# Six runs of V-products for each group of heads become five, with one head scored alone before and after a run

## The chip, the cores and the metric

The kernel runs on one core of a Trainium2 chip. The metric is the device time of one execution in microseconds (us). The core's engines run at the same time and meet at semaphores: TensorE (PE, matmuls into the accumulation banks, eight of 128 x 512 float32), ScalarE (ACT), VectorE (DVE), GpSimd (POOL), and SyncE (SP), which issues DMA transfers.

## The reference: one transformer block, cut to what matters

```
h  = x + Attn(layernorm(x))          # 2048 tokens, D = 512, 32 query heads of 16
h2 = h + FFN(layernorm(h))           # F = 1792, gelu gate

Attn: q = x @ wq (32 heads), k = x @ wk, v = x @ wv (one k, v for all heads)
      p = softmax(q k^T / 4);  o = p @ v;  o @ wo
FFN:  (gelu(x @ w_gate) * (x @ w_up)) @ w_down
```

All arrays are float32. Every query attends to every key.

## The kernel before: what is tiled, staged and ordered

**Attention.** The queries are cut into 4 blocks of 512 tokens, the heads into 8 groups of four, the keys into 16 chunks of 128. For each block, group and chunk there are four scored heads. They are scored in pairs (`scores`, L363): two matmuls with 50 contraction rows each, one in rows 0 to 63 and one in rows 64 to 127 of the array, side by side, into a tile `s` of two banks. ScalarE turns the pair into exponentials with one instruction on 128 x 1024 elements (L374) and writes them into a buffer `p` of the chunk; there are five such buffers. When both pairs of a chunk are done, the V-products (`weigh`, L376) multiply the four heads by the chunk's V, 32 columns wide, side by side into one bank `acc` that collects the 16 chunks of a group. Each V-product is float32 and shows as two matmuls, so a chunk has eight.

A group of heads is thus 32 pairs and 16 chunks; the whole has 1024 pairs and 512 chunks. `n` counts pairs.

**Dense products.** The projection with wo (`pp`), gate and up (`pg`, `pu`) and down (`pd`) of a finished block run between the attention matmuls of the next block (`queue_products`, `rows`, L808). A weight or activation is split in a high and a low part, so a product has three matmuls for each piece of the contraction. The contraction of 128 rows is cut in two halves of 64: the first halves (`firsts`, rows 0 to 63) and the second halves (`seconds`, rows 64 to 127) are two lists of matmuls. One `step` (L837) issues the next of each, side by side, into two different banks; the seconds run `LAG` = 6 steps behind the firsts. A product of 12 or more steps ends with an addition or a copy on VectorE (`done`), which frees the bank, and then up to two further pieces of waiting VectorE work are issued (`side(2)`: the gelu gate, layer norm, transposes). There are three banks for the dense products: one with the firsts, one with the seconds, one being freed or free.

**The order.** TensorE, ScalarE and GpSimd execute in the order in which the program is written, and in the stage of this change VectorE and SyncE too. First comes a prologue with k, v and the first q, then a lead (pairs 0 to 278, loops at L1125 and L1127), in which attention runs beside the remaining q projection and the weights' splitting; there the score tiles have three buffers, later two. After pair 279 the table `CYCLES` sets the order: one entry is (how many chunks a run of V-products takes, the pattern of `s` for a pair and `d` for a step after that run, the pattern when there is no dense work). Three entries make 8 chunks, 16 pairs and 36 steps. Each cycle begins with `before` (tanh instructions, two pieces of side work, a transpose of a normed tile) and `finish(count)`, the run of V-products; then the pattern follows. When the dense list has fewer steps ready than the pattern wants (`idle`), what is ready is issued at once, `catch_up` lets the lone seconds run to their end if the next product is a `pg` or none is left, and the cycle goes on in the third pattern: runs of one chunk with two pairs between them. Such a cycle is called plain here, the other woven. A dense product that starts after a catch-up has its first six firsts alone.

Behind the last run of V-products comes a tail: the last block's projection and feed-forward layer.

## Time and profile before

| what | value |
|---|---|
| three runs | 1395.55, 1395.99 (median), 1398.74 us |
| the profiled execution | 1397.61 us, its span 1395.8 us |
| PE busy | 1379.5 us, 99% of the span |
| ACT busy | 1034.1 us, 74% |
| DVE busy | 651.0 us, 47% |
| granted TensorE clock | 1.000 |
| first dense matmul, last V-product's end | 313.5 us, 1253.6 us |

A timeline row gives the start in us from the span's start, the length in us, the engine, the line, the operation with output and inputs, and how many instructions were merged. Matmul ends are modelled, so the distance between two starts is the safer number. A "step" or a "pair" stands for two matmuls in the two halves of the array.

### The profile page before, as it was taken

The numbers are of one execution on the slowest core, as the hardware profiler recorded it, in microseconds if no ns is written. First come the engines' busy times: TensorE is split into PE (matmuls) and PEld (weight loads), VectorE is DVE, ScalarE is ACT, GpSimd is POOL, SyncE is SP. The second block draws the span as 40 slices with busy tenths as digits, with TensorE's granted clock in tenths as the row PEclk, the third lists the DMA queues.
The fourth block names the chain that finished last, engine by engine and source line by source line (L and its number), as shares of the span: only waits on it lengthen the run. The fifth ranks groups of instructions, "written<-read, shape, count | busy, mean of one in ns | idle before, by whom it ended". The sixth has DMA issues, their size and how long they took to land.

```text
span 1395.8 us, 25287 instructions
## 1 busy us (share of the span) xinstructions
PE 1379.5 (99%) x10406; PEld 753.3 (54%) x10406; DVE 651.0 (47%) x1097; ACT 1034.1 (74%) x1157; POOL 239.8 (17%) x346
## 2 busy tenths in 40 slices
PE   9999999999999999999999999999999999999998
PEld 7533333325555555545555555545555555558886
DVE  7413131314354444548364444448364453546665
ACT  8799999997787777877787777787778777772000
POOL 7576777621000000002000000001000000011000
PEclk9999999999999999999999999999999999999999
DMA  5565776753232333311522433321433333233552
GB/s 163 167 216 184 235 235 233 220 181 133 73 106 74 118 104 103 116 60 46 181 94 81 134 103 103 104 66 31 148 103 104 118 103 103 91 123 126 187 205 94
DMA packets 66783, 180.32 MB, mean 129 GB/s; under 512 B 9672, under 2 KB 9672, under 8 KB 66628
## 3 DMA queue, kind: packets, MB, share of 16 engines
q1 hardware_dynamic: 55324, 143.29, 31.0%
q0 software_dynamic: 10208, 35.26, 7.6%
q8 instruction: 84, 1.38, 0.4%
q14 instruction: 39, 0.32, 0.1%
q10 hardware_dynamic: 1128, 0.07, 0.1%
HBM read 130.87 MB, written 47.45 MB: 128 GB/s over the span
## 4 chain that ended last, share of the span: by engine, by line
PE 94%; ACT 2%; DMA 1%; DVE 1%; issue 1%; SPq 0%; POOL 0%; ACTq 0%; POOLq 0%
PE acc L378 33%; PE s L370 20%; PE pg L827 9%; PE pu L827 8%; PE pd L827 7%; PE pq L219 3%; PE pd L865 3%; PE pg L865 3%; PE pu L865 3%; PE pp L827 2%; ACT p L374 2%; PE pp L929 1%; PE pd_rest L877 1%; DMA x<-in_A_x_dram 1%; PE pk L1327 1%
## 5 line engine op out<-in xcount | busy, mean ns | idle before, releaser
L374 ACT ACTIVATE p<-s 128x1024 f32<-128x1024 f32 x1024 | 959.6, 1037 | 223.7 <-PE s L370 220.6
L378 PE MATMUL acc<-p,v_sb 128*32 128x512 f32 x4096 | 490.0, 598 | 0.0
L370 PE MATMUL s<-qg,kaug 50*128 50x512 f32 x1984 | 388.3, 426 | 4.2 <-ACT p L374 4.1
L370 PEld LDWEIGHTS s<-qg,kaug 50*128 50x128 f32 x1984 | 169.4, 184 | 281.7 <-ACT p L374 123.5
L378 PEld LDWEIGHTS acc<-p,v_sb 128*32 128x32 f32 x4096 | 108.7, 109 | 233.1 <-issue 218.7
L827 PE MATMUL pg<-x2h,w 64*128 64x512 f32 x672 | 175.2, 392 | 0.0
L827 PE MATMUL pu<-x2h,w 64*128 64x512 f32 x672 | 174.5, 392 | 0.0
L827 PE MATMUL pd<-w,gh 64*128 64x512 f32 x624 | 124.7, 394 | 1.9 <-DVE h L615 1.6
L757 DVE TENSOR_TENSOR h<-h,pd 128x512 f32<-128x512 f32 x80 | 55.0, 687 | 140.7 <-PE pd L827 140.6
L137 POOL TENSOR_SCALAR rstd<-mv 128x1 f32<-128x1 f32 x16 | 3.6, 223 | 649.1 <-DVE mv L135 648.8
L827 PEld LDWEIGHTS pg<-x2h,w 64*128 64x128 f32 x672 | 95.5, 186 | 11.4
L827 PEld LDWEIGHTS pu<-x2h,w 64*128 64x128 f32 x672 | 95.7, 186 | 10.8
L827 PE MATMUL pg<-x2l,w 64*128 64x512 f32 x336 | 99.9, 392 | 0.0
L827 PE MATMUL pu<-x2l,w 64*128 64x512 f32 x336 | 99.9, 391 | 0.0
L827 PEld LDWEIGHTS pd<-w,gh 64*128 64x128 f32 x624 | 69.7, 185 | 15.0 <-DVE h L615 2.5
L391 DVE COPY oT<-acc 128x512 f32<-128x512 f32 x32 | 22.1, 692 | 112.5 <-PE acc L378 112.3
L983 ACT ACTIVATE ga<-ga 128x512 f32<-128x512 f32 x14 | 8.8, 632 | 88.5 <-DVE ga L980 88.5
L827 PE MATMUL pd<-w,gl 64*128 64x512 f32 x312 | 72.1, 392 | 0.0
L694 DVE TENSOR_TENSOR g<-g,pg 128x512 f32<-128x512 f32 x42 | 28.8, 685 | 90.8 <-PE pg L827 90.8
L414 DVE RECIPROCAL oc<-oc 128x128 f32<-128x128 f32 x64 | 56.7, 923 | 21.4 <-DMA oc<-acc_d 17.6
L690 DVE COPY g<-pg 128x512 f32<-128x512 f32 x42 | 29.1, 692 | 72.0 <-PE pg L827 72.0
L694 DVE TENSOR_TENSOR u<-u,pu 128x512 f32<-128x512 f32 x42 | 28.8, 686 | 68.6 <-PE pu L827 68.6
(255 smaller groups left out, 1493.1 us busy)
## 6 DMA issues: line engine op xcount, KB each, us to landing
w<-w_d SPq DMA_DIRECT2D x126, 512.0 KB
w<-w_d SPq DMA_DIRECT2D x21, 1024.0 KB
qg<-q_d SPq DMA_DIRECT2D x62, 200.0 KB
q_d<-qh SPq DMA_DIRECT2D x32, 256.0 KB
acc_d<-oT SPq DMA_DIRECT2D x31, 256.0 KB
oc<-acc_d SPq DMA_DIRECT2D x124, 64.0 KB
w_d<-w_0b POOLq DMA_DIRECT2D x14, 512.0 KB, 4.6
w_d<-w_1b POOLq DMA_DIRECT2D x14, 512.0 KB, 3.4
```

What stands on the lines that cost most here:

```text
L219: nc.tensor.matmul(pq, wt[c][:, d, :], xt[:, d, :], start=(n == 0), stop=(n == 3 * DC - 1),)
L370: nc.tensor.matmul(s[:, a, :], kaug[rows, kc * P : (kc + 1) * P], qg[rows, u, :], start=True, stop=True,)
L374: nc.scalar.activation(p[:, 2 * u : 2 * u + 2, :], s, AF.Exp, scale=SCALE)
L378: nc.tensor.matmul(acc[32 * j : 32 * j + 32, :], v_sb[:, kc, :], p[:, j, :], start=(kc == 0), stop=(kc == KC - 1), skip_group_check=True,)
L391: nc.vector.tensor_copy(oT, acc)
L414: nc.vector.reciprocal(oc[:, 1, sl], oc[:, 1, sl])
L690: nc.vector.tensor_copy(half, bank)
L694: nc.vector.tensor_tensor(half, half, bank, op=ALU.add)
L757: nc.vector.tensor_tensor(hs[b, t], hs[b, t], bank, op=ALU.add)
L827: nc.tensor.matmul(bank, lhsT[r], rhs[r], start=(k == 0), stop=(k == n - 1), skip_group_check=True,)
L865: nc.tensor.matmul(bank, lhsT, rhs, start=(i == 0), stop=(i == len(ts) - 1))
L877: nc.tensor.matmul(bank, lhsT, rhs, start=(i == 0), stop=(i == len(ts) - 1))
```

## The change

A group's 16 chunks are taken in five runs of 3, 4, 3, 3 and 3 chunks, with 7, 6, 7, 6, 6 pairs and about 16, 14, 16, 14, 12 steps. The patterns are now made by `woven` and `plain`. A woven cycle ends, where possible (`parted`), with a move `1`: a lone second of the dense products beside the first head of the next pair, which goes into a bank of the dense products (`take_bank`, given back at once). Then comes the run of V-products, and the next cycle begins with a move `2`: a lone first beside the pair's second head, which goes into an `s` tile. Each of the two heads has its own exponential on 128 x 512 elements (`score_half`). `choose` shifts the number of steps by up to two so that a dense product ends 3 to 5 steps ahead of the run, and `EMPTY` = 4 demands as many units of the program's clock since the last end. The lead grows by 5 pairs to 284, and `ENTRY` lets the list begin with its fourth entry. The arithmetic is the same.

```diff
--- before.py
+++ after.py
@@ -45,12 +45,20 @@
 SETTLE = 14
 
 CYCLES = (
-    (3, "ssdddddsdddsddds", "vssvssvs"),
-    (3, "ssdddddsdddsddds", "vssvssvs"),
-    (2, "ssdddddsdddsdddsddds", "ssvssvss"),
+    (3, 7, 16),
+    (4, 6, 14),
+    (3, 7, 16),
+    (3, 6, 14),
+    (3, 6, 12),
 )
 
...
+ENTRY = 3
+
+WHOLE_AT, HALF_AT = (0, 1, 7, 11, 15, 19, 23, 27, 31), (1, 5, 9, 13, 17, 21, 25, 29)
+
+EMPTY = 4
+
...
@@ -820,6 +831,7 @@
                 tag, bank = take_bank(f"{name}_{a}")
                 r = slice(64 * a, 64 * a + 64)
                 for k in range(n):
+                    todo[a] = n - k - 1
                     if a == 0:
                         sent.append(next(source))
                         left[0] -= 1
@@ -830,19 +842,50 @@
                     )
                     if k == n - 1:
                         spare.append(tag)
+                        todo[2] = clock
                         done(a, bank)
                         side(2)
                     yield
 
-        def step(first=True):
+        def step(first=True, second=True):
             nonlocal ahead, clock
             clock += 1
             if first and next(firsts, 0) is None:
                 ahead += 1
-            if ahead > LAG or not first:
-                assert ahead > 0
+            if second and (ahead > LAG or not first) and ahead > 0:
                 next(seconds)
                 ahead -= 1
+
+        def last_end(steps, shift):
+            ends = [0]
+            for first, late in (
+                (todo[0] or 12, 0),
+                (todo[1] or 12 + max(LAG - ahead, 0), shift),
+            ):
+                ends += range(first + late, steps + 1, 12)
+            return max(ends)
+
+        def choose(steps, half):
+            for more in (0, 1, -1, 2, -2):
+                if steps + more - last_end(steps + more, half) in (3, 4, 5):
+                    return steps + more, True
+            return steps, False
+
+        def woven(pairs, steps, half, parted):
+            steps -= half
+            at, moves = (HALF_AT if half else WHOLE_AT)[:pairs], "2" * half
+            while pairs or steps:
+                if pairs and (len(moves) >= at[-pairs] or not steps):
+                    moves, pairs = moves + "s", pairs - 1
+                else:
+                    moves, steps = moves + "d", steps - 1
+            return moves + "1" * parted
+
+        def plain(count, pairs):
+            moves = "s" * (pairs - 2 * count)
+            for i in range(count):
+                moves += "v" + "s" * min(max(pairs - 2 * i, 0), 2)
+            return moves
...
@@ -1058,8 +1101,26 @@
                 cur["p"] = sb.tile([P, 4, T], F32, tag="p", bufs=PB, name=f"p_{i}")
+            return i, u, b, g, kc
+
+        def score(n):
+            i, u, b, g, kc = open_pair(n)
             scores(i, cur["p"], cur["qg"], kc, u)
             if u == 1:
+                pend.append((b, g, kc, cur["p"], acc, n))
+
+        def score_half(n, a):
+            if a == 0:
+                cur["open"] = open_pair(n)
+            i, u, b, g, kc = cur["open"]
+            if a == 0:
+                tag, s = take_bank(f"s_{i}_{u}_0")
+                spare.append(tag)
+            else:
+                s = pss.tile([P, 2, T], F32, tag="s", bufs=2, name=f"s_{i}_{u}_1")[:, 0, :]
+            score_head(s, cur["qg"], kc, u, a)
+            nc.scalar.activation(cur["p"][:, 2 * u + a, :], s, AF.Exp, scale=SCALE)
+            if a == 1 and u == 1:
                 pend.append((b, g, kc, cur["p"], acc, n))
 
         banks.close()
@@ -1073,7 +1134,7 @@
         width = 1
 
 
-        n, lead = 0, 2 * PER + 23
+        n, lead = 0, 2 * PER + 28
         with tc.manual_schedule(engines={mybir.EngineType.SP, mybir.EngineType.DVE}):
             parts = None
             if first:
@@ -1126,9 +1187,9 @@
                 moves[move]()
             while n < lead:
                 pace()
-                if n % 4 == 2 and len(pend) > 2 and n < lead - 1:
+                if n % 4 == 2 and len(pend) > 2 and n < lead - 2:
                     finish(1)
-                elif n % 4 == 0:
+                elif n % 4 == 0 and n < lead:
                     finish(len(pend) - 2)
         assert not outs
         set_banks("ps_rest")
@@ -1164,12 +1225,19 @@
         fixed.enter_context(
             tc.manual_schedule(engines={mybir.EngineType.SP, mybir.EngineType.DVE})
         )
-        for i in range(-((lead - end) // 16)):
+        half, target = False, lead
+        for i in range(-((lead - end) // 32)):
             if first and i in BOUND_LISTS:
                 bound_flag(BOUND_LISTS.index(i))
-            for count, woven, plain in CYCLES:
-                idle = available() < woven.count("d")
+            for count, pairs, steps in CYCLES[0 if i else ENTRY :]:
+                target += pairs
+                steps, parted = choose(steps, half)
+                parted = parted and not scaled_at and target < end
+                idle = available() < steps + parted
                 if idle:
+                    if half:
+                        score_half(n, 1)
+                        n, half = n + 1, False
                     while available():
                         step()
                     if at == len(queue) or queue[at][0].startswith("pg"):
@@ -1181,7 +1249,13 @@
                     finish(count)
                 for key in bent:
                     later.extend(gate(*key))
-                for move in plain if idle else woven:
+                pairs = min(target, end) - n
+                moves = (
+                    plain(count, pairs)
+                    if idle
+                    else woven(pairs - half - parted, steps, half, parted)
+                )
+                for move in moves:
                     if move == "d":
                         step()
                     elif move == "v":
@@ -1189,10 +1263,22 @@
                             prepare_x()
                         finish(1)
                         clock += 4
+                    elif move == "1":
+                        if scaled_at or clock - todo[2] < EMPTY:
+                            step()
+                        else:
+                            step(first=False)
+                            score_half(n, 0)
+                            half = True
+                    elif move == "2":
+                        step(second=False)
+                        score_half(n, 1)
+                        n, half = n + 1, False
                     elif n < end:
                         score(n)
                         n += 1
                         clock += 1
```

The built programs differ in their order on TensorE and VectorE. From the first dense matmul to the last V-product there were 148 runs of V-products: 90 of three chunks, 45 of two, 13 of one. Now there are 133: 20 of four, 89 of three, 24 of one. Ahead of that, in prologue and lead, 96 runs became 98. 96 pairs are scored in two halves. Matmuls of dense products that stand alone because of a catch-up or a restart were 24 and are 48.

**A woven run of V-products, on TensorE**, in the last group of the third query block (`s` score tiles, `acc` the V-products' bank, `p` the exponentials, `pd`, `pg`, `pu` dense products; the digit ahead of a dense name's last number is 0 for a first and 1 for a second). Before:

```order
L827 MATMUL pd_8_1_0_13192<-w_2_4_11759,gh_4_12288 128x512
L827 MATMUL pd_8_0_1_13180<-w_2_5_12603,gh_5_12840 128x512
L370 MATMUL s_0_13206<-qg_7_12540,kaug 128x512 x2
L378 MATMUL acc_7_12909<-p_13126,v_sb 32x512 x4
L378 MATMUL acc_7_12909<-p_13147,v_sb 32x512 x4
L378 MATMUL acc_7_12909<-p_13182,v_sb 32x512 x4
L370 MATMUL s_1_13223<-qg_7_12540,kaug 128x512 x2
L370 MATMUL s_0_13228<-qg_7_12540,kaug 128x512 x2
L827 MATMUL pd_8_1_0_13192<-w_2_4_11759,gh_4_12288 128x512
```

With the change:

```order
L839 MATMUL pg_13_0_13217<-x2h_10276,w_2_13_0_13078 128x512
L839 MATMUL pg_13_1_13245<-x2h_10276,w_2_13_0_13078 128x512
L839 MATMUL pg_13_1_13245<-x2l_10277,w_2_13_0_13078 128x512
L382 MATMUL s_0_0_13259<-qg_7_12699,kaug 128x512
L388 MATMUL acc_7_13068<-p_13154,v_sb 32x512 x4
L388 MATMUL acc_7_13068<-p_13186,v_sb 32x512 x4
L388 MATMUL acc_7_13068<-p_13212,v_sb 32x512 x4
L388 MATMUL acc_7_13068<-p_13239,v_sb 32x512 x4
L839 MATMUL pg_13_0_13217<-x2l_10277,w_2_13_0_13078 128x512
L382 MATMUL s_0_1_13279<-qg_7_12699,kaug 128x512
L382 MATMUL s_1_13282<-qg_7_12699,kaug 128x512 x2
```

The pair ahead of the run and one of the two pairs behind it are now one head beside a lone second, and one head beside a lone first; here the run has four chunks.

**The last gate of a block, on TensorE** (second query block; `gh_6`, `gl_6` are the high and low part of the gate's output for the last two of 14 pieces, and a wait for `DVE_49` is one for VectorE). Before:

```order
L378 MATMUL acc_7_9494<-p_9793,v_sb 32x512 x4
L378 MATMUL acc_7_9494<-p_9815,v_sb 32x512 x4
L378 MATMUL acc_7_9494<-p_9848,v_sb 32x512 [waits Activation_49]
L378 MATMUL acc_7_9494<-p_9848,v_sb 32x512
L378 MATMUL acc_7_9494<-p_9848,v_sb 32x512 [waits Activation_49]
L378 MATMUL acc_7_9494<-p_9848,v_sb 32x512
L370 MATMUL s_0_9877<-qg_7_9125,kaug 128x512 [waits PE_49]
L370 MATMUL s_0_9877<-qg_7_9125,kaug 128x512
L370 MATMUL s_1_9881<-qg_7_9125,kaug 128x512 [waits PE_49]
L370 MATMUL s_1_9881<-qg_7_9125,kaug 128x512
L827 MATMUL pd_11_0_0_9841<-w_1_6_9190,gh_6_9719 128x512 [waits DVE_49]
```

With the change:

```order
L839 MATMUL pd_11_0_0_9985<-w_1_6_9313,gh_6_9909 128x512
L839 MATMUL pd_8_1_1_9954<-w_1_5_9311,gh_5_9567 128x512
L839 MATMUL pd_11_0_0_9985<-w_1_6_9313,gl_6_9910 128x512
L839 MATMUL pd_8_1_1_9954<-w_1_5_9311,gl_5_9568 128x512
L382 MATMUL s_0_10006<-qg_7_9216,kaug 128x512 [waits Activation_49]
L382 MATMUL s_0_10006<-qg_7_9216,kaug 128x512
L839 MATMUL pd_11_0_0_9985<-w_1_6_9313,gh_6_9909 128x512 [waits DVE_49]
L839 MATMUL pd_11_0_1_10011<-w_1_5_9311,gh_5_9567 128x512
L839 MATMUL pd_11_0_0_9985<-w_1_6_9313,gh_6_9909 128x512
L839 MATMUL pd_11_0_1_10011<-w_1_5_9311,gh_5_9567 128x512
L839 MATMUL pd_11_0_0_9985<-w_1_6_9313,gl_6_9910 128x512 [waits DVE_49]
```

The first use of the last gate's output (`gh_6` with a wait for VectorE) stood behind a run of V-products and stands now four rows behind the same product's use of the piece ahead of it, with one pair between.

**The same place on VectorE.** Before:

```order
L712 SCALAR_TENSOR_TENSOR ga_13_9743<-ga_13_9743,g_13_9647 128x512 [waits Activation_49]
L715 TENSOR_TENSOR ga_13_9743<-ga_13_9743,u_13_9741 128x512 [waits DVE_49]
L757 TENSOR_TENSOR h_1_6737<-h_1_6737,pd_8_1_0_9780 128x512 [waits PE_49]
L724 CAST gh_6_9719<-ga_13_9743 128x512 [waits DVE_49]
L728 TENSOR_TENSOR gl_6_9720<-ga_13_9743,gh_6_9719 128x512 [waits DVE_49]
L757 TENSOR_TENSOR h_1_6737<-h_1_6737,pd_8_1_1_9828 128x512 [waits PE_49]
```

With the change:

```order
L767 TENSOR_TENSOR h_1_6808<-h_1_6808,pd_8_1_0_9930 128x512 [waits PE_49]
L722 SCALAR_TENSOR_TENSOR ga_13_9835<-ga_13_9835,g_13_9807 128x512 [waits Activation_49]
L725 TENSOR_TENSOR ga_13_9835<-ga_13_9835,u_13_9877 128x512 [waits DVE_49]
L767 TENSOR_TENSOR h_1_6808<-h_1_6808,pd_8_1_1_9954 128x512 [waits PE_49]
L734 CAST gh_6_9909<-ga_13_9835 128x512 [waits DVE_49]
L738 TENSOR_TENSOR gl_6_9910<-ga_13_9835,gh_6_9909 128x512 [waits DVE_49]
```

The gate's last four operations (`ga`, `ga`, `gh`, `gl`) moved behind one further addition of a down product (`h`) each: the first two stand behind that of `pd_8_1_0`, the last two behind that of `pd_8_1_1`. The same holds in the first and third block.

**Where a block's dense work ends, on TensorE** (`pxt` is the transpose of a normed tile, from which the next block's gate and up products come). Before:

```order
L827 MATMUL pd_8_3_0_7066<-w_0_4_4964,gl_4_5463 128x512
L827 MATMUL pd_8_2_1_6986<-w_0_6_5810,gl_6_6309 128x512
L370 MATMUL s_1_7090<-qg_1_6522,kaug 128x512 x2
L628 MATMUL pxt_3_7094<-ident,xb_3_6804 128x128 x4
L378 MATMUL acc_1_6912<-p_7012,v_sb 32x512 x4
L378 MATMUL acc_1_6912<-p_7038,v_sb 32x512 x4
L378 MATMUL acc_1_6912<-p_7073,v_sb 32x512 x4
L370 MATMUL s_0_7116<-qg_1_6522,kaug 128x512 x2
L370 MATMUL s_1_7120<-qg_1_6522,kaug 128x512 x2
L827 MATMUL pd_8_3_0_7066<-w_0_5_5808,gh_5_6020 128x512
```

With the change:

```order
L839 MATMUL pd_8_3_0_7127<-w_0_6_5871,gl_6_6473 128x512
L839 MATMUL pd_8_3_1_7160<-w_0_5_5869,gl_5_6160 128x512
L839 MATMUL pd_8_3_1_7160<-w_0_6_5871,gh_6_6472 128x512 x2
L839 MATMUL pd_8_3_1_7160<-w_0_6_5871,gl_6_6473 128x512
L839 MATMUL pd_8_3_1_7160<-w_0_6_5871,gh_6_6472 128x512 x2
L839 MATMUL pd_8_3_1_7160<-w_0_6_5871,gl_6_6473 128x512
L638 MATMUL pxt_3_7207<-ident,xb_3_6905 128x128 x4
L388 MATMUL acc_1_6958<-p_7065,v_sb 32x512 x4
L382 MATMUL s_0_7221<-qg_1_6558,kaug 128x512 x2
L382 MATMUL s_1_7225<-qg_1_6558,kaug 128x512 x2
L388 MATMUL acc_1_6958<-p_7092,v_sb 32x512 x4
L382 MATMUL s_0_7234<-qg_1_6558,kaug 128x512 x2
```

The down product `pd_8_3` went on beyond the run of V-products behind the transpose; now it is issued to its end ahead of the transpose, with six lone seconds, and a plain stretch follows. Such a stretch follows here in two blocks.

17 lines of the change are left out of this document (10 added, 7 removed).

## Prediction

> **What bounds the kernel now.** I read the page's busy shares first, then its chain of waits, then TensorE's waits and timeline.
>
> ```profile
> span 1395.8 us, 25287 instructions
> PE 1379.5 (99%) x10406; PEld 753.3 (54%) x10406; DVE 651.0 (47%) x1097; ACT 1034.1 (74%) x1157; POOL 239.8 (17%) x346
> PE 94%; ACT 2%; DMA 1%; DVE 1%; issue 1%; SPq 0%; POOL 0%; ACTq 0%; POOLq 0%
> PE s L370 <- ACT p L374: 1.9, 7, 0.4
> PE pd L827 <- DVE h L615: 1.6, 2, 0.8
> ```
>
> TensorE works 99% of the span and carries 94% of the chain. In the stage from the first dense matmul to the last V-product it waits only 1.9 us for exponentials (seven times, 0.4 at most) and 1.6 us for VectorE (twice). So the time is the sum of TensorE's slots, and a change is worth what it takes from or adds to them. The change keeps every score, V-product and dense matmul; it alters what stands between them and what stands alone.
>
> TensorE's timeline shows the prices. The first four rows are from a stretch of `pp` steps, the rest from a woven cycle.
>
> ```profile
> 335.16 0.39 PE L827 MATMUL pp<-wo_hi,o_hi 64*128 64x512 f32 x2
> ...
> 337.74 0.40 PE L827 MATMUL pp<-wo_hi,o_lo 64*128 64x512 f32 x2
> ...
> 338.20 0.39 PE L827 MATMUL pp<-wo_lo,o_hi 64*128 64x512 f32 x1
> ...
> 339.11 0.39 PE L827 MATMUL pp<-wo_hi,o_lo 64*128 64x512 f32 x1
> ```
> ```profile
> 713.39 0.40 PE L827 MATMUL pg<-x2h,w 64*128 64x512 f32 x2
> 713.86 0.40 PE L370 MATMUL s<-qg,kaug 50*128 50x512 f32 x2
> 714.19 2.78 PE L378 MATMUL acc<-p,v_sb 128*32 128x512 f32 x24
> 716.90 0.73 PE L370 MATMUL s<-qg,kaug 50*128 50x512 f32 x4
> 717.47 0.39 PE L827 MATMUL pu<-x2l,w 64*128 64x512 f32 x1
> ...
> 720.48 0.45 PE L370 MATMUL s<-qg,kaug 50*128 50x512 f32 x2
> 720.86 1.07 PE L378 MATMUL acc<-p,v_sb 128*32 128x512 f32 x8
> ```
>
> A slot (two matmuls side by side) takes (337.74 - 335.16) / 11 = 0.2345 us, a lone matmul (339.11 - 338.20) / 4 = 0.2275: a lone one saves nothing, its partner's half is lost. A run of three chunks takes 716.90 - 714.19 = 2.71. With 0.99 for a run of one (below) a chunk costs (2.71 - 0.99) / 2 = 0.86, and each run 0.13 besides. The pair ahead of a run takes 0.33 to 0.38 (713.86 to 714.19, 720.48 to 720.86) where a slot takes 0.2345, so 0.10 to 0.15 is lost there; the two pairs behind it take 0.57 where two slots take 0.47, another 0.10. **A run's two edges thus cost 0.33 to 0.38 us**, whatever its length.
>
> **Part 1: fewer runs.** The order has 244 runs before the tail, and now 231 (148 and 96, now 133 and 98). 13 x 0.34 = **-4.4 us**, between -4.3 and -4.9. This counts all runs, those of plain stretches and of the lead too.
>
> Behind it lies the assumption that an edge costs the same when a half pair stands at it. The trace of before has no run with a dense matmul at its edge. At 96 of the runs the pair ahead and the first pair behind are replaced. If the 0.10 behind a run, which the first pair's wait for the run would explain, went away there, it would bring 96 x 0.10 = -9.6; as much more is the other end. I take nothing, since matmuls in 64 rows follow matmuls in 128 rows as before.
>
> **Part 2: more lone matmuls.** 24 become 48. Two of them fill what would be one slot, so 24 / 2 = 12 slots more: 12 x 0.23 = **+2.8 us**. TensorE has no gap that hides them.
>
> **Part 3: a longer lead.** The lead gets two more runs of one chunk and five more pairs. The lead's rows give the price:
>
> ```profile
> 303.79 1.06 PE L378 MATMUL acc<-p,v_sb 128*32 128x512 f32 x8
> ...
> 305.62 1.06 PE L378 MATMUL acc<-p,v_sb 128*32 128x512 f32 x8
> ...
> 307.45 1.07 PE L378 MATMUL acc<-p,v_sb 128*32 128x512 f32 x8
> ```
>
> One chunk with two pairs takes 1.83. Twice that and one pair at ScalarE's pace (0.915, below) is 4.57. The stage gets rid of two chunks and five pairs, 2 x 0.86 + 5 x 0.2345 = 2.89, and the edges of two runs, 0.68, are in part 1 already. It leaves **+1.0 us**.
>
> **Part 4: longer plain stretches.** 13 single runs become 24 (their edges are in part 1). The rows are of a plain stretch in the third block:
>
> ```profile
> 930.71 1.07 PE L378 MATMUL acc<-p,v_sb 128*32 128x512 f32 x8
> ...
> 932.55 1.07 PE L378 MATMUL acc<-p,v_sb 128*32 128x512 f32 x8
> 933.54 0.51 PE L370 MATMUL s<-qg,kaug 50*128 50x512 f32 x2
> ...
> 934.24 0.50 PE L370 MATMUL s<-qg,kaug 50*128 50x512 f32 x2 [0.19 <-ACT p L374]
> 934.67 1.07 PE L378 MATMUL acc<-p,v_sb 128*32 128x512 f32 x8
> ...
> 938.62 1.06 PE L378 MATMUL acc<-p,v_sb 128*32 128x512 f32 x8
> ```
>
> The run of one is 933.54 - 932.55 = 0.99. A chunk with its two pairs would need 0.86 + 0.34 + 0.47 = 1.67; here it takes (938.62 - 930.71) / 4 = 1.98, in the lead 1.83, since there is no dense work to fill the time in which ScalarE works. So each plain chunk loses 0.16 to 0.31. For 11 more at 0.2: **+2.2 us**, between 1.8 and 3.4.
>
> **Part 5: the last gate of a block.** The order shows `pd_11_0_0` wanting the last `gh_6` ten slots behind the first pair after the run, in three blocks. VectorE must by then have done, in this order: the addition of `pd_8_1_0`, two `ga`, the addition of `pd_8_1_1`, the cast `gh`.
>
> ```profile
> L757 DVE TENSOR_TENSOR h<-h,pd 128x512 f32<-128x512 f32 x80 | 55.0, 687 | 140.7 <-PE pd L827 140.6
> L715 DVE TENSOR_TENSOR ga<-ga,u 128x512 f32<-128x512 f32 x42 | 29.1, 692 | 1.5
> L712 DVE SCALAR_TENSOR_TENSOR ga<-ga,g 128x512 f32<-128x512 f32 x42 | 28.7, 684 | 0.0
> L724 DVE CAST gh<-ga 128x512 fp32r<-128x512 f32 x42 | 17.5, 418 | 0.3
> ```
> ```profile
> 713.82 0.69 DVE L690 COPY g<-pg 128x512 f32<-128x512 f32 x1 [0.68 <-PE pg L827]
> ```
>
> Count from the run's end. Two pairs take 0.57, then `gh_6` is wanted after 10 slots, at 0.57 + 2.35 = 2.9. The last matmul of `pd_8_1_0` starts one slot after the pairs, at 0.8. An evacuation starts 0.43 after the last matmul's start (713.39 to 713.82), so at 1.2. Then 0.69 + 0.69 + 0.68 + 0.69 + 0.42 = 3.17, and some 0.15 between the five: `gh` is there at 4.55. TensorE, which runs in order, stands still for 1.65 us, and everything behind it. Three blocks make **+5.0 us**. Bounds: nothing, if VectorE's work were spread otherwise than the issue order says; 2.0 each, 6.0, if `gl` too comes late.
>
> **Part 6: stalls that lose their cause.** The 1.6 us for `h L615` were two waits of a down product for a block's `h` behind stream transposes; the order now has the end of that block's work ahead of a plain stretch. Twice more a down product waited some 0.3 for a bank just being emptied:
>
> ```profile
> 913.32 0.39 PE L827 MATMUL pd<-w,gl 64*128 64x512 f32 x2
> 913.85 0.50 PE L827 MATMUL pd<-w,gh 64*128 64x512 f32 x2
> ```
>
> 0.53 where a slot takes 0.2345. Together 1.6 + 0.3 + 0.3, and some 0.2 that follow them: **-2.4 us**, between 0 and -2.7.
>
> **Part 7: banks for the halves.** A half pair takes a bank at least 5, mostly 6.5 to 9.5 slots after its last product ended, that is 1.2 us or later. The copy above ends 0.43 + 0.69 = 1.12 after the last matmul's start. So the usual case just fits, and a late evacuation (VectorE is 47% busy) stalls TensorE. I take **+0.5 us**, between 0 and 2: 6 of 96 at 0.35.
>
> ScalarE has two costs that I put at nothing.
>
> ```profile
> 717.44 4.69 ACT L374 ACTIVATE p<-s 128x1024 f32<-128x1024 f32 x5 [1.48 <-PE s L370]
> ```
> ```profile
> 37.37 0.57 ACT L1351 ACTIVATE vT<-pk 128x512 f32<-128x512 f32 x1
> 37.84 0.66 ACT L1347 ACTIVATE kaug<-pk,bias 128x512 fp32r<-128x512 f32 x1
> ```
>
> An exponential of a pair comes every (4.69 - 1.03) / 4 = 0.915 us, under the 0.938 of four slots, and waits for TensorE after a run. An instruction on 512 elements comes about 0.47 after the one before it, so a split pair costs ScalarE some 0.03 to 0.1 more, 96 times; it has 26% of the span free. The fourth chunk's V-products start 3 x 0.86 behind the first's, so its exponentials have that much longer. Without this cover each run of four would wait up to one exponential, 0.9.
>
> **The sum.** -4.4 + 2.8 + 1.0 + 2.2 + 5.0 - 2.4 + 0.5 = **+4.7 us**. The profiled execution took 1397.61 us (span 1395.8), 1.6 above the median of the runs; 1397.6 + 4.7 on its scale is 1400.7 on the median's.
>
> **The rivals.**
>
> *The stalls are covered* (0.20). If parts 4 and 5 cost nothing, it is -4.4 + 2.8 + 1.0 - 2.4 + 0.5 = -2.5, or 1393.5; 1392.5 with the higher price of an edge. For it speaks that VectorE is busy only 47%; against it that the gate's five operations stand in one chain, and that a plain chunk shows 1.98 in the rows.
>
> *The edges become cheaper* (0.12). With 0.10 less at 96 runs the time is 1400.7 - 9.6 = 1391.1, faster than before. For it: the first pair behind a run is issued with a wait for TensorE itself. Against it: the 0.10 stand behind runs of one and of three alike, as a change of the array's shape would have it.
>
> *The halves' banks come late* (0.14). If the evacuations, which now share VectorE with the gate in fewer and longer cycles, missed half of the 96 by 0.1, and the edges cost 0.03 more, it would be +4.7 + 4.8 - 0.5 + 2.9, or 1408; half of it 1404. The point from which it decides is 5 slots, 1.17 us, against 1.12.
>
> *A second row half's loads show* (0.03). Move `1` puts a lone second next to a step's second, both in rows 64 to 127. If a load of weights could not run under a matmul in the same rows, each of 96 lone seconds would cost one load:
>
> ```profile
> L370 PEld LDWEIGHTS s<-qg,kaug 50*128 50x128 f32 x1984 | 169.4, 184 | 281.7 <-ACT p L374 123.5
> ```
>
> 96 x 0.184 = 17.7, or 1418. Against it: the five lone seconds from 338.20 to 339.11, all in rows 64 to 127, come 0.2275 apart, no longer than a slot, so their loads are hidden.
> [...]
>
> **How the numbers follow.** The forecast has 0.48, its own range 1397 to 1404; 0.03 are left for what I don't see. The predicted time is 1400.7. The range 1391.5 to 1405 leaves out the loads, part of the late banks and a part of the cheaper edges. A measurement of this kernel tells 0.3% from no change, 4.2 us: faster is under 1391.8, slower over 1400.2. Faster: 0.08 of the cheaper edges, 0.04 of the covered stalls, 0.03 of the unseen, 0.15 in all. Slower: 0.27 of the forecast, 0.12 of the late banks, 0.03 of the loads, 0.42. Within: 0.43.
>
> **What would show it.** Right: runs still cost 0.13 and 0.20 at the edges (half pairs included); three waits of `pd` for `gh`, 1.4 to 2 us each, in TensorE's waits; plain chunks 1.83 to 2.0 apart; the `h` wait gone; lone matmuls 0.2275 apart. Wrong: `gh` waits under 0.5 us, waits of half scores for VectorE in sum over 2 us, new waits of V-products for ScalarE in runs of four, or slots other than 0.2345 next to a half pair.

## The result: 1.65% slower

The changed kernel took 1419.72 us (median of five runs, 1418.47 to 1420.26), the kernel before 1395.99 us. The ratio is 1.0165, with a 95% interval of 1.015 to 1.018. The forecast was 1400.7, the range ended at 1405: the direction was as forecast, the size was 23.7 us instead of 4.7.

The page of the changed kernel, its busy shares and its chain, and then TensorE's waits in the stage (engine, line, what it waited for, us in total, times, longest):

```profile
span 1418.5 us, 25378 instructions
PE 1394.4 (98%) x10406; PEld 755.2 (53%) x10406; DVE 653.2 (46%) x1097; ACT 1038.6 (73%) x1253; POOL 240.1 (17%) x346
PE 92%; DVE 3%; ACT 2%; issue 1%; DMA 1%; POOL 1%; SPq 0%; ACTq 0%; DVEq 0%; POOLq 0%
```
```profile
PE s L382 <- ACT p L378: 4.9, 12, 0.8
PE s L382 <- DVE h L628: 3.8, 4, 1.7
PE pd L839 <- DVE gh L734: 3.7, 3, 1.4
```

TensorE has the same 10406 matmuls, but is busy 14.9 us longer, and VectorE has risen from 1% to 3% of the chain. Two waits are new: scores that wait for an addition `h` on VectorE, and down products that wait for the last `gh`. The two make 7.5 us; waits for exponentials grew by some 2.6 us, and the 1.6 us for the old `h` are gone. Most of the loss is in no list of waits.

So I laid the matmuls' starts beside the program's order, slot by slot, and compared each with the prices of the prediction (0.2345 a slot, 0.86 a chunk, 0.33 a run's edges). The span is 22.7 us longer: 4.5 in the lead, 18.2 in the stage. What is above those prices rose from 10.8 to 34.5 us in the stage. The places:

| place | predicted, us | found, us |
|---|---|---|
| 13 runs fewer | -4.4 | -4.3 |
| 12 slots more for lone matmuls | +2.8 | +2.8 |
| longer lead, net | +1.0 | +0.9 |
| plain chunks, 11 more | +2.2 | +3.5 |
| last gate, three blocks | +5.0 | +5.0 |
| old stalls gone | -2.4 | -3.4 |
| half pairs' banks late | +0.5 | +5.9 |
| V-products at half the granted clock | none | +3.2 |
| the regular woven cycles (ScalarE's pace, in part only argued) | 0 | +5.0 |
| a dozen places at the blocks' ends, 0.1 to 0.9 each | none | +4.6 |

They add up to 23.2, against 22.7 of the span. The last row is what is left of the slots' sum, not a cause.

**The half pairs' banks and the clock.** Here is TensorE's timeline of the second query block, then VectorE's, then two windows (start and end; PE, PEld, DVE, ACT and POOL busy with their instructions; granted clock; DMA share; GB/s):

```profile
642.36 0.62 PE L382 MATMUL s<-qg,kaug 50*128 50x512 f32 x2
642.83 0.40 PE L839 MATMUL pp<-wo_hi,o_hi 64*128 64x512 f32 x1
644.92 0.64 PE L382 MATMUL s<-qg,kaug 50*128 50x512 f32 x1 [1.70 <-DVE h L628]
645.50 4.26 PE L388 MATMUL acc<-p,v_sb 128*32 128x512 f32 x24
649.69 0.49 PE L839 MATMUL pp<-wo_hi,o_hi 64*128 64x512 f32 x1
```
```profile
641.06 0.68 DVE L625 TENSOR_TENSOR h<-pp,xb 128x512 f32<-128x512 f32 x1
641.66 2.49 DVE L659 STREAM_TRANSPOSE xt<-xb 32x128 f32<-32x128 f32 x8
644.18 0.69 DVE L628 TENSOR_TENSOR h<-h,pp 128x512 f32<-128x512 f32 x1
```
```profile
646.00:647.00 1.00, 1.00 (x8) 0.20 (x4) 0.96 (x4) 0.20 (x1) 0.69 (x2) 0.50 0.00 0
647.00:648.00 1.00, 1.00 (x8) 0.20 (x4) 0.96 (x4) 0.00 (x0) 0.00 (x0) 0.50 0.00 0
```

The half score at 644.92 goes into a bank that the addition L628 has to empty, and on VectorE eight stream transposes, 2.49 us, stand ahead of that addition. TensorE stands still for 2.1 us between two starts. Then the run of three chunks takes 649.69 - 645.50 = 4.19 us, not 2.71: the granted clock is 0.50 for 3.4 us from 645.12 on. The same happens once more, at 973 us; two further waits of 0.7 are without a fall of the clock.

**ScalarE.** TensorE behind another run, and ScalarE at that time:

```profile
724.62 0.73 PE L382 MATMUL s<-qg,kaug 50*128 50x512 f32 x3
...
725.66 0.39 PE L839 MATMUL pu<-x2h,w 64*128 64x512 f32 x1
...
725.89 0.44 PE L382 MATMUL s<-qg,kaug 50*128 50x512 f32 x2
726.17 0.39 PE L839 MATMUL pg<-x2h,w 64*128 64x512 f32 x1
```
```profile
725.18 0.60 ACT L1122 ACTIVATE p<-s 128x512 f32<-128x512 f32 x1 [1.75 <-PE pu L839]
725.68 4.69 ACT L378 ACTIVATE p<-s 128x1024 f32<-128x1024 f32 x5
```

The sixth slot, at 725.89, takes 0.28. Its tile is the half pair's, whose exponential ends at 725.78; the slot is drawn out by 0.05, and no wait is listed, since by the profile the matmul before it ends only at 726.05. This is so behind 95 runs. In the cycle of 12 steps for 6 pairs the last pairs seem to come too early for ScalarE as well, 0.17 us in each of 19 cycles: 494.02 - 493.72 is 0.30, 494.37 - 494.02 is 0.35, where a slot has 0.2345.

```profile
493.72 0.39 PE L839 MATMUL pu<-x2l,w 64*128 64x512 f32 x1
...
494.02 0.72 PE L382 MATMUL s<-qg,kaug 50*128 50x512 f32 x3
494.37 0.39 PE L839 MATMUL pu<-x2h,w 64*128 64x512 f32 x1
```

The 5.0 us in the table are the regular woven cycles of both kernels against each other; the 19 cycles of 12 steps hold some 3.2 of them.

### The profile page after: what moved, and what is told of

Its sections match the earlier page's. It is cut to its first block, busy times and chain, and to the rows that moved or that the text cites. A ratio compares the mean times of both kernels' runs of the same rounds, so it can differ in the third digit from the quotient of the medians.

```text
span 1418.5 us, 25378 instructions
## 1 busy us (share of the span) xinstructions
PE 1394.4 (98%) x10406; PEld 755.2 (53%) x10406; DVE 653.2 (46%) x1097; ACT 1038.6 (73%) x1253; POOL 240.1 (17%) x346
## 4 chain that ended last, share of the span: by engine, by line
PE 92%; DVE 3%; ACT 2%; issue 1%; DMA 1%; POOL 1%; SPq 0%; ACTq 0%; DVEq 0%; POOLq 0%
PE acc L388 33%; PE s L382 18%; PE pg L839 9%; PE pu L839 9%; PE pd L839 8%; PE pq L227 3%; PE pd L908 3%; PE pg L908 3%; PE pu L908 3%; ACT p L378 2%; PE pp L839 1%; PE pp L972 1%; DVE xt L659 1%; PE pd_rest L920 1%; PE pk L1413 1%
## 5 line engine op out<-in xcount | busy, mean ns | idle before, releaser
L378 ACT ACTIVATE p<-s 128x1024 f32<-128x1024 f32 x928 | 869.6, 1045 | 61.0 <-PE s L382 58.0
L382 PE MATMUL s<-qg,kaug 50*128 50x512 f32 x1984 | 422.9, 426 | 10.8 <-ACT p L378 6.6
L382 PEld LDWEIGHTS s<-qg,kaug 50*128 50x128 f32 x1984 | 186.8, 184 | 214.9 <-ACT p L378 129.1
L1122 ACT ACTIVATE p<-s 128x512 f32<-128x512 f32 x192 | 120.4, 628 | 178.7 <-PE s L382 141.3
L839 PE MATMUL pu<-x2h,w 64*128 64x512 f32 x672 | 193.5, 398 | 0.1
L839 PE MATMUL pg<-x2h,w 64*128 64x512 f32 x672 | 191.1, 396 | 0.0
L839 PE MATMUL pg<-x2l,w 64*128 64x512 f32 x336 | 106.1, 396 | 0.0
L839 PE MATMUL pd<-w,gl 64*128 64x512 f32 x312 | 78.5, 398 | 0.0
L839 PEld LDWEIGHTS pg<-x2l,w 64*128 64x128 f32 x336 | 50.3, 186 | 16.5 <-issue 10.9
```

The costliest lines, as they stand in the source:

```text
L378: nc.scalar.activation(p[:, 2 * u : 2 * u + 2, :], s, AF.Exp, scale=SCALE)
L382: nc.tensor.matmul(s, kaug[rows, kc * P : (kc + 1) * P], qg[rows, u, :], start=True, stop=True)
L839: nc.tensor.matmul(bank, lhsT[r], rhs[r], start=(k == 0), stop=(k == n - 1), skip_group_check=True,)
L1122: nc.scalar.activation(cur["p"][:, 2 * u + a, :], s, AF.Exp, scale=SCALE)
```

## The experiments

All but the ladders start from the changed kernel: seven turn one thing in it, and three combine several of these edits. The arithmetic is the same in all. Their times are compared with runs of the kernel before on the same chip, and their traces with the changed kernel's by the length of the stage, from the first dense matmul to the last V-product's start: 939.6 us before, 957.8 changed. Where the number of half-clock runs (runs of V-products at a granted clock of 0.50) differs, it is given, 1.5 to 1.7 us each: with nearly the same stall ahead of them (2.08 to 2.10 us) some traces show such a run and others don't.

### Which half pairs cost

```diff
-                        if scaled_at or clock - todo[2] < EMPTY:
+                        if scaled_at or clock - todo[2] < EMPTY or queue[at - 1][0].startswith("pp") or queue[at - 1][0].endswith(("_8_2", "_8_3")):
                             step()
```

> The changed kernel, but no half pair is begun while the projection or the two down products behind it run: six pairs of 96 are scored whole, beside a step, and nothing else moves. Theory A (a few halves wait long, for a bank whose addition stands behind stream transposes on VectorE, and the two longest waits are followed by V-products at half the granted clock): the four waits of 2.3, 2.2, 0.7 and 0.7 us and the slow runs of 4.2 and 4.4 us (2.71 otherwise) go, some 9.5 us in all, time about 1410. Theory B (the loss is spread over all 96 halves): a sixteenth of the loss, under 2 us, time 1418 to 1420. Theory C (the two slow runs have a cause of their own, not the stall ahead of them): the waits go, the runs of 4.2 us stay, time about 1413.

Measured: 1414.15 us, ratio 1.013 (1.0113 to 1.0147), stage 952.0, that is 5.8 less than the changed kernel's. Six pairs of 96 carry that: theory B is out. The four long waits are gone and so are both half-clock runs, so theory C, by which the runs would have stayed, is out too. Here is the run at the place of the first, at its usual length, and what came back of the gain:

```profile
643.20 2.78 PE L388 MATMUL acc<-p,v_sb 128*32 128x512 f32 x24
...
649.76 0.50 PE L839 MATMUL pp<-wo_hi,o_hi 64*128 64x512 f32 x1 [0.57 <-DVE h L625]
```

Now the next projection waits for its bank, 0.73 above a slot in each of two blocks. These are 1.5 of the 3.3 us that came back (9.1 in the table, 5.8 gained); the rest was not located. Theory A had the mechanism, and 5.8 of its 9.5 us.

### The order on VectorE alone

```diff
                         done(a, bank)
-                        side(2)
+                        side(0 if a == 0 and name in ("pp_1_1", "pp_2_1", "pp_1_3", "pp_2_3") else 2)
```

> The changed kernel with all 96 half pairs; only VectorE's order differs: after the first half of the second and the fourth projection of a block no stream transposes are issued, so that the second half's addition of the projection before comes right behind. Theory A (a half pair's bank waits for an addition that stands behind eight stream transposes, and the half clock follows from that stall): the waits of half scores for h (3.8 us listed, 5.9 against a slot's time) and both slow runs (3.2 us) go, 8 to 9 us, part of which can come back as waits for a later transpose or h as in the first experiment (5.6 of 9.5 were kept there): time 1411 to 1414. Theory B (a half pair's bank is late for another reason, such as the copy in front): the waits stay, 1418 to 1420.

Measured: 1414.55 us, ratio 1.0118 (1.0101 to 1.0135), stage 950.9, 6.9 less. (Its profiled execution has one stall of 5.9 us in the lead, so only its stage is compared.) VectorE now does one addition behind the other, and the run is 2.71 again:

```profile
649.40 0.68 DVE L625 TENSOR_TENSOR h<-pp,xb 128x512 f32<-128x512 f32 x1
650.19 0.69 DVE L628 TENSOR_TENSOR h<-h,pp 128x512 f32<-128x512 f32 x1
```

With all 96 half pairs in place the waits for L628 are 0.6 us in all, not 3.8. It is the eight transposes ahead of the addition that cost, not the half pair as such. One half pair in each of two blocks still comes 0.8 late.

### The last gate

```diff
                 for key in bent:
-                    later.extend(gate(*key))
+                    if key[1] == FC - 1:
+                        for part in gate(*key):
+                            part()
+                    else:
+                        later.extend(gate(*key))
```

> The changed kernel with the last gate's four VectorE operations of a block issued right behind the run of V-products, ahead of the addition of the next down product. Theory A (the three waits for gh are that order's price): the three waits of 1.3 to 1.5 us for gh and the 0.2 to 0.4 that follow each go, -5 us, time about 1414.7. Theory B (VectorE then only waits for the tanh and is late for the down products' banks instead): the waits turn into waits for h of similar length, 1418 to 1421.

First the changed kernel itself at this place, VectorE and TensorE, the second query block:

```profile
935.07 0.69 DVE L767 TENSOR_TENSOR h<-h,pd 128x512 f32<-128x512 f32 x1 [3.61 <-PE pd L839]
935.67 0.68 DVE L722 SCALAR_TENSOR_TENSOR ga<-ga,g 128x512 f32<-128x512 f32 x1
936.39 0.69 DVE L725 TENSOR_TENSOR ga<-ga,u 128x512 f32<-128x512 f32 x1
937.00 0.68 DVE L767 TENSOR_TENSOR h<-h,pd 128x512 f32<-128x512 f32 x1
937.60 0.42 DVE L734 CAST gh<-ga 128x512 fp32r<-128x512 f32 x1
```
```profile
933.84 0.73 PE L382 MATMUL s<-qg,kaug 50*128 50x512 f32 x4
...
938.08 0.72 PE L839 MATMUL pd<-w,gh 64*128 64x512 f32 x4 [1.18 <-DVE gh L734]
```

The chain runs as the prediction had it: the addition 1.23 us behind the run's end, `gh` used at 4.24 (predicted 1.2 and 4.55).

With the edit: 1415.94 us, ratio 1.0141 (1.0125 to 1.0158), stage 952.7, 5.1 less, of which some 1.6 is one half-clock run that did not happen here. The edit's own 3.5 are the 5.0 of the three waits less what came back, above all in the first block, where the bank of a down product is now late:

```profile
PE pd L839 <- DVE h L767: 0.8, 1, 0.8
```

This is theory A in two blocks, and a piece of theory B in the first.

### ScalarE's pace

```diff
-..., (1, 5, 9, 13, 17, 21, 25, 29)
+..., (1, 6, 9, 13, 17, 21, 25, 29)
```

> The changed kernel with one number changed: behind a half pair the third score tile of a cycle comes one slot later (position 6, not 5). Theory A (that pair waits for ScalarE to have done the half pair's second exponential, 0.046 us in each of 95 cycles, though no wait is listed): -4.4 us, time about 1415.3, and the sixth slot behind a run takes 0.235 instead of 0.28. Theory B (the 0.28 is the price of going from dense products to scores at that place, whatever stands there): no change, 1419 to 1420, the 0.28 moves by one slot.

Measured: 1418.74 us, ratio 1.0161 (1.0144 to 1.0178), stage 957.0, 0.8 less, both half-clock runs there. The sixth slot takes 0.23 and the tenth 0.268 instead: the loss went on to the next pair, four slots on, which neither theory had. The exponential that frees that tile ends 2.08 us behind the run's end, the slot starts at 2.21 and is drawn out by 0.03, as if a tile came free 0.16 behind the end of its exponential; the same 0.16 fits the first place. So the next experiment makes all three pairs later.

```diff
-..., (1, 5, 9, 13, 17, 21, 25, 29)
+..., (1, 6, 10, 14, 18, 21, 25, 29)
```

> The changed kernel with the third, fourth and fifth score tile behind a half pair each one slot later (positions 6, 10, 14, 18), where the second experiment moved the third alone. Theory A (ScalarE, which starts 0.57 us behind the run's end with a half pair of 0.49 and then takes 0.905 for a pair, gives a tile back 0.16 after its instruction's end, at 1.33, 2.24 and 3.15 us; the tiles at positions 5, 9 and 13 want 1.28, 2.26 and 3.20, in the second experiment 1.50, 2.21, so the wait went to the next tile; at 6, 10 and 14 they want 1.50, 2.44, 3.38): the sixth slot takes 0.235 and no other takes over, 12 slots behind a run take 2.91 instead of 2.956, in all -4, time about 1415.5. Theory B (the 0.05 comes back wherever dense matmuls and scores meet): 12 slots at 2.94 or more, 1418 to 1420.

Measured: 1420.13 us, ratio 1.0158 (1.0139 to 1.0177), stage 956.0, 1.8 less, of which 1.5 is a half-clock run that did not happen. The twelve slots behind a run do take 2.915 instead of 2.956, close to theory A's 2.91; yet most of the 4 us did not stay. In the four longer kinds of cycle the median loss went from between 0.02 and 0.06 to between 0.00 and 0.05, in those of 12 steps it rose from 0.21 to 0.28. Where the pairs stand within a cycle is hardly what costs: what the first twelve slots gain, the end of the cycle loses. That the end is another of ScalarE's limits is argued, not shown.

```diff
     (3, 7, 16),
-    (3, 6, 14),
-    (3, 6, 12),
+    (3, 6, 13),
+    (3, 6, 13),
```

> The changed kernel with the last two cycles of 14 and 12 steps made 13 and 13. Theory A (the cycle with 12 steps for 6 pairs is bound by ScalarE, 0.17 us in each of 23): these 0.17 go, -3.9 us, time about 1415.8. Theory B (ScalarE has enough free time, the 0.17 is an edge's price): no change, 1419 to 1420.

Measured: 1418.25 us, ratio 1.0154 (1.0137 to 1.0171), stage 954.4, 3.4 less, one half-clock run fewer (1.6). The median loss of the cycles in question fell from 0.21 and 0.05 to 0.06 each, some 2.8 us over them; a wait for a weight's load that was not there before, 1.7 us, took part of it. Theory A in the cycle, half of its size in the time: by the ratio alone the edit can't be told from no change.

### Without half pairs

```diff
-                        if scaled_at or clock - todo[2] < EMPTY:
+                        if True:
                             step()
```

> The changed kernel without half pairs: every pair is scored whole, a step takes the place of each move. The order then has 144 runs in the stage instead of 133, 41 of them single ones in plain stretches (24), with the same number of slots. Theory A (half pairs cost by late banks, the clock and ScalarE's first pair behind a run, some 10 to 14 us; a plain chunk costs 0.33 for its run and 0.3 of waiting): -12 + 11 x 0.33 + 17 x 0.3 = -3, time about 1416. Theory B (half pairs pay for themselves, since without them ScalarE runs dry in a run of four): waits for exponentials grow by over 10 us, 1425 or more.

Measured: 1440.13 us, ratio 1.0307 (1.029 to 1.0324), stage 974.8, 17.0 more. Theory A fell clearly, and theory B named the wrong cause. The waits in its stage:

```profile
PE s L382 <- ACT p L378: 9.6, 29, 0.7
PE pd L839 <- DVE gh L734: 7.7, 3, 2.6
```

Waits for exponentials are 4.7 us longer, not 10. The long waits for `h L628` and both half-clock runs, 9.1 us in the changed kernel, are gone here as well (the clock falls once, behind the first gate's wait), so other places lose some 26 us more. The 11 runs more are 11 x 0.33 = 3.6 us; the last gate costs 2.7 to 2.8 in each block instead of 1.3 to 1.5, 4 us; the 17 plain chunks more are 6 us. The rest, about half, lies in the woven cycles and at the blocks' ends and was not traced to a cause: the 18 cycles of 13 steps, for one, lose 0.38 each. So the half pairs, whatever they cost, save more in this order, in which 17 single runs fewer are needed with them.

### Three and four edits at once

The edits of the order on VectorE, the last gate and the 13 steps together:

> The changed kernel with three edits at once: the order on VectorE of the fifth experiment, the last gate's operations at once (fourth), the last two cycles of 13 steps (third). If the three losses add up as measured alone (8.5 or 5.6, 5.1 and 3.4 in the stage): 1419.7 less 14 to 17, time 1403 to 1406, still slower than before. If they hide one another (TensorE waits for the next thing instead): 1408 or more.

Measured: 1406.11 us, ratio 1.0061 (1.0044 to 1.0078), stage 943.8, 14.0 less, with no half-clock run. They add up (6.9, 3.5 and 1.8 without the half-clock runs counted twice make 12.2, and the three together bring somewhat more). Nearly two thirds of the changed kernel's loss are mended, and it is still 0.6% slower than before: the longer lead (0.9 us net in the table), the plain chunks (3.5) and the lone matmuls (2.8) are among what is left.

With the later positions as well:

> The sixth experiment's three edits and the ninth's positions. Additive: 1.0061 of the time before, less 4 us (0.0029): ratio 1.003, stage 940 us. If the later positions collide with the cycles of 13 steps, where ScalarE was the bound: ratio 1.006.

Measured: 1406.39 us, ratio 1.0052 (1.0035 to 1.007), stage 945.2, no gain; TensorE's waits for weights' loads rose from 0.8 to 2.4 us, which would leave a stage about as long as the sixth's without them. Of the 4 us expected of the later positions nothing shows. No version here beats the kernel before.

### The lead

```diff
-        n, lead = 0, 2 * PER + 28
+        n, lead = 0, 2 * PER + 23
-ENTRY = 3
+ENTRY = 2
```

> The tenth experiment's kernel with the lead of the kernel before (279 pairs instead of 284, entering the list of cycles one entry earlier). The order has 135 runs in the stage and 96 ahead of it, 231 in all as with 284 pairs, 26 single ones (24) and 5 slots more in the stage. Theory A (the longer lead costs what its 4.57 us are above the stage's price for the same work): -1.0, and +0.4 for two more single runs in plain stretches: 0 to -1 us against the tenth. Rival (the lead's work is as cheap as the stage's): no change or +0.5. The lead's end in the trace should come 4.5 us earlier in both.

Measured: 1431.64 us, ratio 1.0237 (1.022 to 1.0254). The lead ends at 313.5, 4.5 us earlier as expected, and then the stage is 975.1 instead of 945.2. Neither theory had it:

```profile
PE acc L388 <- DVE oT L401: 19.3, 21, 2.6
```

With 279 pairs a run holds the last chunks of one group and the first of the next, and the next group's first V-product waits within the run until VectorE has copied the bank `acc`, 0.9 us on average, 21 times: 19.3 of the 29.9 us. With 284 pairs a group ends where a run ends. The lead's length is thus tied to the five runs; what it costs, 0.9 us net in the table, is part of their price.

### What the granted clock does after a stall

```diff
                 if a == 0:
                     half = db.tile([P, T], F32, tag=tag, bufs=2, name=f"{tag}_{b}_{f}")
+                    for _ in range(late.get((b, f), 0) if k == 0 else 0):
+                        nc.vector.tensor_copy(half, bank)
                     nc.vector.tensor_copy(half, bank)
```

This is the kernel before, with `late` a table of repeats for twelve gate products: 2 to 7 in the first ladder, 4 to 12 in the second.

> The kernel before, with the first copy of some gate products repeated 2 to 7 times on VectorE (0.69 us each), so that their bank comes free late and TensorE stands still for steps of a ladder, some 0.5 to 4 us, with nothing else of the change in it. Theory A (the granted clock falls to 0.5 for some 3 us after a stall of TensorE of over about 1.7 us, with dense work as with V-products): each longer step of the ladder is followed by rows at half the pace, each shorter one by none. Theory B (the fall had to do with half pairs or V-products): the clock stays at 1.00 throughout. Its time is that of the stalls, 1410 to 1440, and says nothing else.

The first ladder (1401.71 us, one run) made only one long stall, 2.22 us between two starts, and the clock stayed at 1.00.

> The kernel before with longer repeated copies than in the eighth run (5 to 12 and 4 to 10), which had one stall of 1.8 us without a fall of the clock. Theory A (the clock falls after a stall of some length over 1.8 us, whatever work stands around it): stalls of 2.5 us and more are followed by 3 us at half the pace, those of 1.8 or less by none. Theory B (length is not enough; in the changed kernel the matmuls ahead of the stall were thin, lone ones with gaps, so that a stretch of some 3 us had little work in it): stalls up to about 2.5 us among dense work are followed by no fall, and only those of 3 us or more are, if any. The time says nothing else (1405 to 1440).

The second (1445.55 us, one run) had eleven. Two of nearly the same length, among the same kind of dense work, and the windows behind them:

```profile
751.73 0.40 PE L831 MATMUL pu<-x2h,w 64*128 64x512 f32 x1
753.86 0.49 PE L831 MATMUL pu<-x2h,w 64*128 64x512 f32 x1 [1.74 <-DVE g L694]
```
```profile
754.90:755.90 1.00, 1.00 (x11) 0.54 (x11) 0.97 (x2) 1.00 (x2) 0.00 (x0) 1.00 0.00 0
```
```profile
1098.51 0.40 PE L831 MATMUL pu<-x2h,w 64*128 64x512 f32 x1
1100.68 0.62 PE L831 MATMUL pu<-x2h,w 64*128 64x512 f32 x1 [1.78 <-DVE g L694]
```
```profile
1101.70:1102.70 1.00, 1.00 (x8) 0.82 (x6) 0.96 (x2) 0.51 (x1) 0.00 (x0) 0.50 0.00 0
```

2.13 us between starts and no fall; 2.17 us, and the clock at 0.50. Both theories fall: neither the length alone nor the work around it decides. Over all the traces of this case, by the distance between two starts, up to 1.90 us in the stage, never a fall; in the stage or the lead, 2.08 to 2.24 us, 10 times of 17; 2.86 to 2.97 us, 5 of 7; 3.2 us and more, 4 of 4. The very same stall of the changed kernel shows it in the ninth experiment: 2.09 us from 644.06, and this time the run behind it has its 2.71.

```profile
644.06 0.39 PE L839 MATMUL pp<-wo_hi,o_hi 64*128 64x512 f32 x1
646.14 0.50 PE L382 MATMUL s<-qg,kaug 50*128 50x512 f32 x1 [1.70 <-DVE h L628]
646.57 2.78 PE L388 MATMUL acc<-p,v_sb 128*32 128x512 f32 x24
```

What goes with a fall in these traces is where the stall lies on a grid that the falls themselves show. In each trace they start whole multiples of 3.413 us apart: in the changed kernel at 645.12 and 976.21, 331.09 apart, which is 97 pieces; in the second ladder all nine do (three of them, by the windows' clock, at 1100.90, 1158.94 and 1189.66: 17 and 9 pieces). Each lasts one piece, 3.41 us, once two and once three. From trace to trace the grid lies differently: the fall behind the stall at 643 us starts at 645.12 in the changed kernel, at 645.93 in the second experiment and at 644.87 in the fourth. Here are the two pieces at 0.50 in the changed kernel:

```profile
645.12:648.53 3.41, 3.41 (x17) 0.79 (x20) 3.25 (x10) 0.60 (x1) 0.79 (x2) 0.50 0.00 0
976.21:979.62 3.41, 3.41 (x20) 0.87 (x16) 3.07 (x10) 0.33 (x1) 0.85 (x3) 0.50 0.00 0
```

Of the 28 stalls of 2.08 us and more, 17 have at least that much in one piece, and behind each of them the clock was at 0.50 from the end of that piece on. Seven are cut by the grid so that no piece holds more than 1.70 us, and none of these brought a fall; of the four between (1.79 to 1.98 us) two did. The ladder's stall at 751.73 is cut into 1.02 and 1.11 us, the one at 1098.51 lies in one piece; the ninth experiment's is cut into 1.28 and 0.81. Not every fall had one long stall ahead of it: in the leads of the third and the ninth experiment the clock fell at 286.1 and 286.9 us with no stall above 1.11 us between two starts near it, and these leads are some 1.5 us longer than the changed kernel's, which has the same waits and no fall. That several waits in one piece add up there is a guess, not shown.

## Why the prediction was wrong

**Right, with their sizes.** The runs (part 1): the edges are as before, half pairs included. A run of four takes 717.21 - 713.63 = 3.58, 4 x 0.86 + 0.13:

```profile
713.63 3.64 PE L388 MATMUL acc<-p,v_sb 128*32 128x512 f32 x32
717.21 0.73 PE L382 MATMUL s<-qg,kaug 50*128 50x512 f32 x3
```

The lone matmuls (part 2), the lead (part 3: 4.48 us for 4.57) and the last gate (part 5: 1.5 to 1.7 a block for 1.65, with the order of its operations as forecast) came as worked out. The stalls that went (part 6) were worth 3.4 for 2.4, more than its bound of 2.7. Part 4 was 3.5 for 2.2, just above its upper bound of 3.4. The rivals of cheaper edges and of covered stalls did not happen, nor did the loads of weights in the same rows: at 1418 that rival named nearly the measured time, by a mechanism that the trace does not show: the slot with a lone second and a half score takes 0.328 with the run's edge behind it, where a whole pair took 0.329 before.

**The step that failed first: part 7.** It took 1.12 us for an evacuation and gave the late ones 0.35 us, 6 times (which makes 2.1, its upper bound, and not the 0.5 of the sum). The evacuations that matter there are not copies of a gate product but the projection's additions, and ahead of those the order puts eight stream transposes, 2.49 us. The row of the old stall for `h L615`, behind just such transposes, was quoted in the prediction and used for part 6 only. Four waits are 5.9 us, and behind two of them the granted clock was 0.50, 3.2 us, which no part of the sum had. The fifth experiment shows both by changing VectorE's order alone. The rival "the halves' banks come late" had the place, and a price for half of the 96; it is four of 96, and long.

**The step that failed second: ScalarE at nothing.** The prediction compared ScalarE's 0.915 for a pair with 0.938 for four slots and its 26% of free time with its extra work. But a woven cycle begins with ScalarE 0.57 us behind TensorE, and the tile of the half pair comes free another 0.60 + 0.16 us later, the 0.16 an estimate from the end times of the second experiment; the short cycle asks for six pairs in 18 slots, 3 slots a pair. An average says nothing on that. That the cycle of 12 steps asks too much is shown by the third experiment in the cycles' lengths, though not in the time; that the sixth slot is drawn out by the same engine rests on its end times in two kernels, and moving it gave nothing.

**What stays open.** The 4.6 us around the blocks' ends were only located, in some dozen places. So were the losses in the woven cycles without half pairs, and the cause of the 0.05 at the sixth slot is argued from end times. Whether five runs could pay with an order made anew for VectorE and ScalarE was not tried.

## What to carry to other kernels

When a new use is found for a buffer "that is free by then", look up which instruction frees it at each of the places, and what its engine has ahead of that one (here eight transposes, 2.49 us); the mean delay of the common case is no bound: four half pairs of 96 made 5.9 us. An engine with a quarter of its time free can still hold up a cycle, as ScalarE seems to here: it was 73% busy, and the cycles of 12 steps lost 0.21 us each, where those of 13 in the third experiment lost 0.06. Work out its chain from the cycle's first input, not its share. And price a stall of TensorE with what can follow it: 17 stalls here that had 2.08 us or more in one piece of the grid were each followed by a granted clock of 0.50, and a run of V-products at that clock took 1.5 to 1.7 us longer.

## What the runs showed of the hardware that was not expected

In these traces the granted clock fell to 0.50 only at points of a fixed grid of 3.413 us, and for whole pieces of it while the program went on: it did so after a stall of 2.08 us between two starts in one piece, and not after one of 2.97 that the grid cut in two. In the stage it never fell after a stall of up to 1.90 us; in the lead two falls came with waits of 1.11 us at most, several in one piece. A matmul slot was drawn out by 0.05 us with no wait listed (725.89 to 726.17, where a slot takes 0.2345), while the profile lets the matmul before it end at 726.05: only the distances between starts show it. A lone matmul in rows 64 to 127 beside another product's in rows 0 to 63 took no longer than a whole pair in its place: 0.328 us with a run's edge behind it, where the pair took 0.329 before.
